# Second quarter's weight columns by direct transfers of three queues, its row cleared earlier, and the middle of each transform moved into a spare half bank

## The chip, the cores and the metric

The kernel runs on one core of a Trainium2 chip. The metric is the device time of the launch in microseconds (us); smaller is better. A run's median is compared, and the profile is of one further execution.

## The reference, cut to what matters

```python
def _attn_ref(x):                       # x: (8, 3008, 256) float32
    X = np.fft.fft(x, axis=1)
    X = np.fft.fft(X, axis=2)
    return X.real.astype(np.float32)

def _moe_ref(x, w_in, w_out):           # x: (24064, 256); w_in: (256, 2048); w_out: (2048, 256)
    h = x @ w_in
    g = h * np.cos(h)
    return (g @ w_out).astype(np.float32)
```

The output of the first is reshaped to 24064 rows and is the input of the second.

## The kernel before, in words

**The two parts.** The first part is a Fourier transform written as matmuls. Each of the 8 batches is folded (sums and differences of mirrored rows and columns), multiplied with small cosine and sine matrices (tiles `pz`, `pm` and `pb` in PSUM), and passes through DRAM (`zd`) to be turned. The second part runs over steps. A step is one batch, one of 6 groups of up to 256 columns of the transformed input, and one of 8 pairs of 128-row blocks of `w_in`. A step has two halves, `u` = 0 and 1, so there are 8 x 6 x 8 x 2 = 768 half-steps, numbered `k`. The transform's last matmul is folded into the weights: `w_in`, in four quarters of 512 columns, is multiplied with a cosine and a sine matrix (`CS`) in the opening, into `WC` and `WS`. `weights(e, q)` does that on TensorE in the tile `pw`, and `keep_weights` copies it out on VectorE.

**The row and the columns.** Row 0 of `WS` is used in another way than the rest: it must stand as columns, one per 128-row block, in the tile `wn` (16 columns, four for each quarter). Then row 0 of `WS` is set to zero (`clear_wn`, on GpSimd, L653) before TensorE multiplies with it. Before the change the four quarters get their columns in three ways: quarter 0 by four direct transfers from SBUF to SBUF (L998, two by SyncE, two by GpSimd); quarter 1 by four small matmuls that turn the row (`turn_wn`, L634) and a copy on VectorE (`keep_wn`, L644); quarters 2 and 3 by a transfer to DRAM and one back (`send_wn` L650, `load_wn` L656).

**A half-step.** ScalarE writes `nb * wn[:, f] + 0.25` into a PSUM tile `H` (`seed`, L707), TensorE adds two matmuls (`mm1`, L726, with `WC` and then `WS`), ScalarE doubles (`act_e`, L738), VectorE makes the mirrored half (`dve_h`, L742), ScalarE rounds (`act_round`, L754), VectorE takes the fraction (`dve_frac`, L758), ScalarE takes the sine (`act_sin`, L764), and VectorE multiplies (`dve_g`, L768). After two halves GpSimd forms sums and differences of the blocks (`sums`, L784 to L791, tile `S`). Seven matmuls a step, `mm2` (L817, tile `M`), multiply by `w_out`, whose blocks are combined in advance on GpSimd (`combine_w2`, L692). Seven sums need three and a half PSUM banks: the second half of the fourth `M` bank is not used. `mm2` of a step runs five to six half-steps after its first half.

**The order.** The program is written in one order, and each engine keeps its own part of it. So an instruction that waits holds whatever stands behind it on its engine, DMA issues included. `H` has four banks in turn, and `M` four. The other transforms' matmuls borrow `H` banks that are free for a moment (`borrow`).

**The middle of a transform.** For batches 1 to 7, the matmuls of a transform are set between those of the batch before it. `pairs` lists at which step a `pair_half` runs (TensorE into `pz`, then ScalarE copies by `keep_z`). Three half-steps after the first pair of a batch, `middle` (L456) multiplies the middle rows and the ends: ten small passes into `pm`, which VectorE has first set to zero (`clear_middle`, L442), and ScalarE copies it to `zm` (L1096).

**Loads and stores of the opening.** SyncE's queue carries, in this order around the change: columns 1 and 3 of quarter 0; quarters 2 and 3 of `w_in` (`load_w`); half of `w_out` (`load_w2`); eight stores of `z` (`store_z`, L473); the rest of `w_out` and a part of the matrix `BJ`; the third quarter's row (`send_wn(2)`); loads of `z` (`load_z`, L506); `load_wn(2)`. `keep_busy` (L672) issues matmuls on ones whose result nobody reads, while TensorE would wait.

Of the kernel before, what the change touches and what calls it, by code (L numbers as in the profile page):

```python
# [131 lines left out]
def kernel(  # L132
# [7 lines left out]
    nc = tc.nc  # L140
# [106 lines left out]
    def load_bj(c0, c1, eng=nc.sync):  # L247
        eng.dma_start(out=BJ[:, c0:c1], in_=B_dr.ap()[:, c0:c1])
# [4 lines left out]
    def load_w2(f0, f1, eng=nc.sync):  # L253
        eng.dma_start(
            out=w2.rearrange("p (q c) -> p q c", c=ND)[:, 2 * f0 : 2 * f1],
            in_=moe_w_out.rearrange("(q p) c -> p q c", p=128)[:, 2 * f0 : 2 * f1],
        )
# [9 lines left out]
    WS = cpool.tile([128, NDFF], FP, tag="WS", name="WS")  # L267
# [12 lines left out]
    def borrow(name, k=0):  # L280
        return ppool.tile([128, 512], FP, tag=f"H{(turn[0] + k) % 4}", bufs=1, name=name)
# [155 lines left out]
        small.append(dict(out=zv[:, 0, :, 0], in_=zr[:, :, 0]))  # L437
        small.append(dict(out=zv[:, 1, :, 0].rearrange("y (q s) -> y q s", s=2), in_=zq[:, p]))

    def clear_middle():  # L440
        pm = borrow("pm")[:, 0:144]
        nc.vector.memset(pm, 0.0)  # L442
        return pm

    def middle(pm):
        xv = xm.rearrange("r (q h s) -> r h q s", h=2, s=2)
        LZ, LM, LE0, LO0 = (L2[:, 64 * q : 64 * q + 64] for q in range(4))
# [20 lines left out]
    def store_z(p, j0=0, j1=NJ, engs=(nc.sync, nc.sync)):  # L468
        half, q = divmod(p, 2)
        zd, zs = take_zd(0, half), zps[p][:, 0:1024]  # L470
        for e in range(2):
            p0 = 16 * e + XP * q
            engs[e].dma_start(  # L473
                out=zd[p0 : p0 + XP, 256 * j0 : 256 * j1].rearrange("i (y d) -> y i d", d=128),
                in_=zs[64 * e + 2 * j0 : 64 * e + 2 * j1, :].rearrange("y (i d) -> y i d", d=128),
            )
# [82 lines left out]

    doubles = {}  # L560
    pairs = {}
    middles = set()
    per = NG * 8

    def transform(b):
        todo = {}

        def at(o, *call):
            todo.setdefault(o, []).append(call)

        for p in range(4):
            sh = (5, 3, 3, 0)[p] if b == 1 else 5 if p == 0 else 0
            o = 8 * p + sh
            if p < 2:
                at(2 if b == 1 else p, turn_x, b, p)
            at(1 + p if b > 1 else max(2, 1 + p), load_xx, b, p)
            at(5 + p + (3 if b == 1 else 0), take_middle, b, p)
            for k in range(2):
                at(o + 6 + k, fold_x, b, p, k)
                at(o + 9 + k, fold_z, b, p, k)  # L580
            pairs[per * (b - 1) + o + 9] = b, p
            at(o + 11, patch_z, b, p)
            at(o + 12, store_pair, b, p)
            if p == 0:
                for e in range(2):
                    at(10 + e, fold_ends, e)
                middles.add(per * (b - 1) + o + 10)
                at(o + 12, store_ends, b)
        at(23, load_z, b, 0)
        at(39, load_z, b, 1)  # L590
        for i in range(3):
            doubles[per * (b - 1) + (44, 46, 47)[i]] = b, (2 * i, 2 * i + 1)
        return todo
# [34 lines left out]
        W = WS if e else WC  # L628
        copy(out=W[:, 512 * n : 512 * n + 512], in_=pw)

    def turn_wn(n, pw):
        for k in range(4):
            f = 512 * n + 128 * k
            nc.tensor.matmul(  # L634
                pw[:, k : k + 1],
                lhsT=WS[0:1, f : f + 128],
                rhs=ones[0:1, 0:1],
                start=k == 0,
                stop=True,
                skip_group_check=True,  # L640
            )

    def keep_wn(n, pw):
        copy_v(out=wn[:, 4 * n : 4 * n + 4], in_=pw[:, 0:4])  # L644

    wds = {}

# [343 lines left out]
    copy_v(out=wrow, in_=WS[0:1, 0:256])  # L991
    pw.append(weights(0, 0, "H"))
    keep_weights(0, 0, pw[1], copy_v)
    for n in (512, 256):
        keep_busy(pds[0], n, False)
    for k in range(4):
        eng = nc.sync if k % 2 else nc.gpsimd
        eng.dma_start(out=wn[:, k : k + 1], in_=WS[0:1, 128 * k : 128 * k + 128])  # L998
    clear_wn(0)
    for q in (2, 3):  # L1000
        load_w(q)
    load_w2(0, 2)
    load_w2(2, 4)
    for p in (1, 2, 0, 3):
        store_z(p, 4)
    load_w2(4, 6)
    load_bj(256, 512)
    load_w2(6, 8)
    opening = {
        0: ((combine_w2, 0, 2), (clear_wn, 1)),  # L1010
        2: ((load_bj, 512, NJ * 64), (combine_w2, 2, 4)),
        3: ((combine_w2, 4, 6, 0, 2),),
        4: ((combine_w2, 4, 6, 2, 4), (load_z, 0, 0, 8), (load_z, 0, 1, 8)),
# [34 lines left out]
    for k in range(2 * n + LAG):  # L1048
        t, u = divmod(k, 2)
        d, v = divmod(k - LAG, 2)  # L1050
        cur, prev, old, nxt = unit(k), unit(k - 1), unit(k - 2), unit(k + 1)
        done = step(d)
        full = step(d if v else d - 1, True)
        if cur:
            if k % (2 * per) == 0:
                todo = transform(cur.s.b + 1) if cur.s.b + 1 < NB else {}
            if k >= AHEAD:
                mm1(cur, 0)
                act_e(cur)
            if k == 0:  # L1060
                for h in (cur, nxt):
                    mm1(h, 0)
                    seed_first(h)
                    act_e(h)
                spread_nb(0)
            if k < AHEAD - 1:
                mm1(cur, 1)
        pair = None if u else pairs.pop(t, None)
        double = None if u else doubles.pop(t, None)
        pm = clear_middle() if u and t in middles else None  # L1070
        if old:
            dve_g(old)
            if old.u:
                sums(old.s)
        if done:
            order = (0, 1, 5, 4, 3, 2, 6) if done is steps[-1] else range(7)
            mm2(done, 4 * v, 4 * v + (1 if pair or double else 3), order)
        if pair:
            pz = [borrow("pz"), borrow("pz", 1)]
            for q in range(2):  # L1080
                pair_half(*pair, q, pz[q])
            mm2(done, 4 * v + 1, 4 * v + 3, order)
        if double:
            pbs = [borrow("pb"), borrow("pb", 1)]
            kept = second_half(*double, pbs)
            mm2(done, 4 * v + 1, 4 * v + 3, order)
        if pm is not None:
            middle(pm)
        if full and full is not steps[-1]:
            take_m(full, 1 if v else 3, nc.vector)  # L1090
        if nxt and 0 < k < AHEAD - 1:
            seed(nxt)
        if prev:
            act_round(prev)
        if pm is not None:
            nc.scalar.copy(out=zm, in_=pm)  # L1096
        if pair:
            keep_z(*pair, 0, pz[0])
        if double:
            keep_b(double[1], kept[0], 0, pbs[0])  # L1100
        if nxt and k >= AHEAD - 1:
            seed(nxt)
        if full and full is not steps[-1]:
            take_m(full, 0 if v else 2, nc.scalar)
        if prev:
            dve_frac(prev)
        if k + 1 in range(2, AHEAD):
            mm1(nxt, 0)
            act_e(nxt)
        if k < 5:  # L1110
            pw.append(weights(*((1, 1), (0, 1), (1, 2), (0, 2), (1, 3))[k]))
        if k == 4:
            pw.append(weights(0, 3))
        if k == 1:
            turn_wn(1, pw[2])
        copy_small()
        if prev:
            act_sin(prev)
        if pair:
            keep_z(*pair, 1, pz[1])  # L1120
        if double:
            keep_b(double[1], kept[0], 1, pbs[1])
            if double != (0, (1,)):
                send_nb(double[1], *kept)
        if cur and k >= AHEAD - 1:
            mm1(cur, 1)
        if done and v == 0:
            mm2(done, 3, 4, order)
        if cur:
            dve_h(cur)  # L1130
        if k < 6:
            e, q = ((1, 1), (0, 1), (1, 2), (0, 2), (1, 3), (0, 3))[k]
            keep_weights(e, q, pw[k + 2], copy_v)
        if k == 1:
            keep_wn(1, pw[2])
        if k == 2:
            send_wn(2)
            load_z(0, 0, 4, 8)
            load_wn(2)
            load_z(0, 1, 4, 8)  # L1140
        if k == 4:
            send_wn(3)
            nc.sync.dma_start(out=L2, in_=L2_dr.ap())
            load_wn(3)
        if k in (5, 7):
            clear_wn((k - 1) // 2)
        if k < 2:
            for o in range(2):
                mix_weights(2 + k, o, nc.gpsimd)
        if u == 0:  # L1150
            continue
        for i in range(6):
            s = step(t - 4 - i, True)
            if s:
                combine_m(s, i)
        for sg, lag in ((0, 8), (1, 10)):
            s = step(t - lag, True)
            if s:
                store_out(s, sg)
        for call in opening.pop(t, ()):  # L1160
            call[0](*call[1:])
        for call in todo.pop(t % per, ()):
            call[0](*call[1:])
# [31 lines left out]
```

## Time and profile before

| | us |
|---|---|
| median of 3 runs | 1917.05 (1915.54 to 1918.67) |
| the profiled execution | 1915.97 |
| its span, first to last instruction | 1914.2 |
| mean granted TensorE clock | 0.999 |

The profile names engines PE (TensorE), PEld (its weight loads), DVE (VectorE), ACT (ScalarE), POOL (GpSimd) and SP (SyncE); a `q` behind the name is the engine's queue of DMA issues. A line of the timeline has the start, the duration, the engine, the source line, the operation, output and inputs with shapes, the number of instructions merged, and in brackets how long the engine had been idle and who ended that. A float32 matmul shows as two passes.

### The profile page before, as it was taken

To read this page: it belongs to the slowest core of one execution; us is meant where nothing else is said; L and a number is where in the kernel's file an instruction comes from. 1 tells how busy PE (TensorE), PEld (TensorE's weight loads), DVE (VectorE), ACT (ScalarE), POOL (GpSimd) and SP (SyncE) were. 2 spreads that over 40 slices of the span, in tenths; PEclk is the share of its full clock that TensorE was granted. 3 is DMA by queue.
4 is the path that set the end of the run, shared out by engine and by line. 5 is a ranking of instruction groups with operands and counts; after the bars stand their busy time and mean duration, and the time that the engine had idled before them with its cause. 6 is when DMAs were issued, how large, how long until landed. Compare 5 with 4: busy or idle time off the path is not lost.

```text
span 1914.2 us, 32347 instructions
## 1 busy us (share of the span) xinstructions
PE 1904.4 (99%) x10410; PEld 1658.9 (87%) x10410; DVE 1463.8 (76%) x2543; ACT 1493.3 (78%) x3354; POOL 1442.3 (75%) x1784
## 2 busy tenths in 40 slices
PE   9999999999999999999999999999999999999998
PEld 4988889888988889888898888988889888898887
DVE  6777777778777777777777777777777777788787
ACT  3777777778787777788777887778777887778775
POOL 6878768887688776888768886688867888666775
PEclk9999999999999999999999999999999999999999
DMA  7612224122231224221252212502116021210001
GB/s 209 162 30 38 49 60 110 27 42 42 73 92 30 40 41 103 61 44 30 40 123 43 46 24 41 142 21 50 29 34 151 16 51 23 40 25 14 12 15 30
DMA packets 173222, 107.96 MB, mean 56 GB/s; under 512 B 112928, under 2 KB 152702, under 8 KB 171984
## 3 DMA queue, kind: packets, MB, share of 16 engines
q1 hardware_dynamic: 170488, 103.33, 24.0%
q8 instruction: 84, 1.38, 0.3%
q10 hardware_dynamic: 1848, 1.28, 0.3%
q0 software_dynamic: 720, 1.30, 0.2%
q14 instruction: 82, 0.67, 0.1%
HBM read 68.59 MB, written 48.39 MB: 61 GB/s over the span
## 4 chain that ended last, share of the span: by engine, by line
PE 99%; DMA 1%; DVE 0%; POOL 0%; issue 0%; ACTq 0%; ACT 0%; SPq 0%; POOLq 0%; DVEq 0%
PE M L817 60%; PE H L726 34%; PE pz L403 2%; PE pb L521 2%; DMA xp<-in_x_dram 0%; PE pz L323 0%; PE pw L618 0%; PE pm L456 0%; DMA z<-zd 0%; DMA zd<-zs 0%; DVE cb L885 0%; PE H L713 0%; PE po L915 0%; POOL xf L306 0%; PE pn L557 0%
## 5 line engine op out<-in xcount | busy, mean ns | idle before, releaser
L784 POOL TENSOR_TENSOR S<-r 128x512 f32<-128x512 f32 (+1 forms) x383 | 474.9, 1240 | 380.4 <-DVE r L768 317.7
L764 ACT ACTIVATE r<-r 128x512 f32<-128x512 f32 (+1 forms) x768 | 476.6, 621 | 246.4 <-DVE r L758 244.5
L758 DVE SCALAR_TENSOR_TENSOR r<-r,H 128x512 f32<-128x512 f32 (+1 forms) x768 | 518.9, 676 | 158.3 <-ACT r L754 133.4
L817 PE MATMUL M<-S,VX 128*128 128x256 f32 (+1 forms) x2304 | 626.6, 377 | 0.0
L768 DVE SCALAR_TENSOR_TENSOR r<-H,r 128x512 f32<-128x512 f32 (+1 forms) x768 | 519.0, 676 | 121.1 <-ACT r L764 79.3
L817 PEld LDWEIGHTS M<-S,VX 128*128 128x128 f32 x2304 | 434.0, 190 | 71.2 <-issue 22.7
L726 PE MATMUL H<-pq,WC 128*128 128x256 f32 (+1 forms) x1536 | 453.3, 377 | 0.0
L726 PE MATMUL H<-pq,WS 128*128 128x256 f32 (+1 forms) x1536 | 451.7, 376 | 0.6 <-POOL WS L653 0.6
L754 ACT ACTIVATE r<-H 128x512 f32<-128x512 f32 (+1 forms) x768 | 447.4, 583 | 0.2 <-DVE H L742 0.2
L742 DVE TENSOR_TENSOR H<-ew,H 128x256 f32<-128x256 f32 (+1 forms) x768 | 324.9, 423 | 147.3 <-PE H L726 90.9
L817 PE MATMUL M<-r,w 128*128 128x256 f32 (+1 forms) x1536 | 388.0, 375 | 0.0
L707 ACT ACTIVATE H<-nb,wn 128x256 f32<-128x256 f32 (+1 forms) x766 | 365.9, 478 | 2.0
L738 ACT ACTIVATE ew<-H 128x256 f32<-128x256 f32 (+1 forms) x768 | 287.2, 374 | 99.4 <-PE H L726 95.1
L817 PEld LDWEIGHTS M<-r,w 128*128 128x128 f32 x1536 | 300.6, 197 | 27.7 <-PE pw L618 0.8
L726 PEld LDWEIGHTS H<-pq,WC 128*128 128x128 f32 x1536 | 283.4, 190 | 45.2 <-ACT H L707 7.6
L726 PEld LDWEIGHTS H<-pq,WS 128*128 128x128 f32 x1536 | 290.0, 190 | 36.0 <-POOL WS L653 1.5
L790 POOL TENSOR_TENSOR S<-S,r 128x256 f32<-128x256 f32 (+1 forms) x383 | 275.4, 719 | 30.1
L791 POOL TENSOR_TENSOR S<-r,S 128x256 f32<-128x256 f32 (+1 forms) x383 | 274.8, 718 | 30.0
L817 PE MATMUL M<-r,VX 128*128 128x256 f32 (+1 forms) x768 | 225.4, 375 | 0.0
L817 PE MATMUL M<-S,w 128*128 128x256 f32 (+1 forms) x768 | 225.4, 375 | 0.0
L817 PEld LDWEIGHTS M<-S,w 128*128 128x128 f32 x768 | 150.5, 196 | 14.4
L817 PEld LDWEIGHTS M<-r,VX 128*128 128x128 f32 x768 | 146.0, 190 | 14.4
(95 smaller groups left out, 887.1 us busy)
## 6 DMA issues: line engine op xcount, KB each, us to landing
out_dram<-ob SPq DMA_DIRECT2D x724, 32.0 KB
xp<-in_x_dram SPq DMA_DIRECT2D x119, 128.0 KB
xp<-xr SPq DMA_DIRECT2D x112, 128.0 KB
z<-zd SPq DMA_DIRECT2D x56, 192.0 KB
xr<-in_x_dram SPq DMA_DIRECT2D x14, 752.0 KB
zd<-zs SPq DMA_DIRECT2D x98, 96.0 KB
nb<-nd SPq DMA_DIRECT2D x23, 256.0 KB
wr<-in_moe_w_in_dram SPq DMA_DIRECT2D x4, 512.0 KB
```

What stands on the lines that cost most here:

```text
L707: nc.scalar.activation(out=h.H[:, 0:T], in_=s.nb[:, 0:T], func=AF.Copy, bias=0.25, scale=wn[:, f : f + 1])
L726: nc.tensor.matmul(h.H[:, 0:T], lhsT=W[:, 128 * f : 128 * f + 128], rhs=s.pq[:, e * 256 : e * 256 + T], start=False, stop=True, skip_group ...
L738: nc.scalar.mul(out=h.ew[:, 0:T], in_=h.H[:, 0:T], mul=2.0)
L742: nc.vector.tensor_tensor(out=h.H[:, T : 2 * T][:, ::-1], in0=h.ew[:, 0:T], in1=h.H[:, 0:T], op=ALU.subtract)
L754: nc.scalar.activation(out=r, in_=y, func=AF.Copy, bias=BIG, scale=1.0)
L758: nc.vector.scalar_tensor_tensor(out=r, in0=r, scalar=-BIG, in1=y, op0=ALU.add, op1=ALU.subtract)
L764: nc.scalar.activation(out=r, in_=r, func=AF.Sin, bias=0.0, scale=SIN_SCALE)
L768: nc.vector.scalar_tensor_tensor(out=r, in0=y, scalar=-0.25, in1=r, op0=ALU.add, op1=ALU.mult)
L784: tt(out=sv[:, 0:2], in0=qv[:, 1:2].to_broadcast([128, 2, T]), in1=qv[:, 0:4:3], op=ALU.subtract,)
L790: tt(out=sv[:, 2], in0=sv[:, 1], in1=gv[:, 0, 0], op=ALU.subtract)
L791: tt(out=sv[:, 3], in0=gv[:, 1, 0], in1=sv[:, 2], op=ALU.add)
L817: nc.tensor.matmul(acc[key][m // 2][:, 256 * (m % 2) : 256 * (m % 2) + T], lhsT=w, rhs=a, start=first, stop=s.fp == 7, skip_group_check=True,)
```

## The change

- Quarter 1's columns (4 to 7 of `wn`) come by four direct transfers: column 4 by ScalarE, 6 and 7 by SyncE, 5 by GpSimd. They are issued in half-step 0, after the row is copied out. The turning matmuls and their copy go.
- `clear_wn(1)` stands at the end of half-step 1 ahead of `combine_w2(0, 2)`, not behind it.
- Six of the eight stores of `z`, two loads of `w_out` and one of `BJ` move on SyncE's queue behind columns 6 and 7.
- One more filler matmul of 512 columns stands ahead of the first steps.
- The middle of a transform is computed directly behind the first pair of its batch, three half-steps earlier, into the spare half of the fourth `M` bank. The memset of `pm` goes. In that step the last of the seven sums is taken ahead of the pair.

```diff
--- before.py
+++ after.py
@@ -437,11 +437,6 @@
         small.append(dict(out=zv[:, 0, :, 0], in_=zr[:, :, 0]))
         small.append(dict(out=zv[:, 1, :, 0].rearrange("y (q s) -> y q s", s=2), in_=zq[:, p]))
 
-    def clear_middle():
-        pm = borrow("pm")[:, 0:144]
-        nc.vector.memset(pm, 0.0)
-        return pm
-
     def middle(pm):
         xv = xm.rearrange("r (q h s) -> r h q s", h=2, s=2)
         LZ, LM, LE0, LO0 = (L2[:, 64 * q : 64 * q + 64] for q in range(4))
@@ -559,7 +554,6 @@
 
     doubles = {}
     pairs = {}
-    middles = set()
     per = NG * 8
 
     def transform(b):
@@ -584,7 +578,6 @@
             if p == 0:
                 for e in range(2):
                     at(10 + e, fold_ends, e)
-                middles.add(per * (b - 1) + o + 10)
                 at(o + 12, store_ends, b)
         at(23, load_z, b, 0)
         at(39, load_z, b, 1)
@@ -628,20 +621,8 @@
         W = WS if e else WC
         copy(out=W[:, 512 * n : 512 * n + 512], in_=pw)
 
-    def turn_wn(n, pw):
-        for k in range(4):
-            f = 512 * n + 128 * k
-            nc.tensor.matmul(
-                pw[:, k : k + 1],
-                lhsT=WS[0:1, f : f + 128],
-                rhs=ones[0:1, 0:1],
-                start=k == 0,
-                stop=True,
-                skip_group_check=True,
-            )
-
-    def keep_wn(n, pw):
-        copy_v(out=wn[:, 4 * n : 4 * n + 4], in_=pw[:, 0:4])
+    def move_wn(k, eng):
+        eng.dma_start(out=wn[:, k : k + 1], in_=WS[0:1, 128 * k : 128 * k + 128])
 
     wds = {}
 
@@ -991,23 +972,18 @@
     copy_v(out=wrow, in_=WS[0:1, 0:256])
     pw.append(weights(0, 0, "H"))
     keep_weights(0, 0, pw[1], copy_v)
-    for n in (512, 256):
+    for n in (512, 512, 256):
         keep_busy(pds[0], n, False)
     for k in range(4):
-        eng = nc.sync if k % 2 else nc.gpsimd
-        eng.dma_start(out=wn[:, k : k + 1], in_=WS[0:1, 128 * k : 128 * k + 128])
+        move_wn(k, nc.sync if k % 2 else nc.gpsimd)
     clear_wn(0)
     for q in (2, 3):
         load_w(q)
     load_w2(0, 2)
     load_w2(2, 4)
-    for p in (1, 2, 0, 3):
-        store_z(p, 4)
-    load_w2(4, 6)
-    load_bj(256, 512)
-    load_w2(6, 8)
+    store_z(1, 4)
     opening = {
-        0: ((combine_w2, 0, 2), (clear_wn, 1)),
+        0: ((combine_w2, 0, 2),),
         2: ((load_bj, 512, NJ * 64), (combine_w2, 2, 4)),
         3: ((combine_w2, 4, 6, 0, 2),),
         4: ((combine_w2, 4, 6, 2, 4), (load_z, 0, 0, 8), (load_z, 0, 1, 8)),
@@ -1067,35 +1043,37 @@
                 mm1(cur, 1)
         pair = None if u else pairs.pop(t, None)
         double = None if u else doubles.pop(t, None)
-        pm = clear_middle() if u and t in middles else None
         if old:
             dve_g(old)
             if old.u:
                 sums(old.s)
         if done:
             order = (0, 1, 5, 4, 3, 2, 6) if done is steps[-1] else range(7)
+            if pair and pair[1] == 0:
+                order = (0, 1, 2, 3, 6, 4, 5)
             mm2(done, 4 * v, 4 * v + (1 if pair or double else 3), order)
         if pair:
             pz = [borrow("pz"), borrow("pz", 1)]
             for q in range(2):
                 pair_half(*pair, q, pz[q])
+            if pair[1] == 0:
+                pm = acc[done.b, done.grp][3][:, 256:400]
+                middle(pm)
             mm2(done, 4 * v + 1, 4 * v + 3, order)
         if double:
             pbs = [borrow("pb"), borrow("pb", 1)]
             kept = second_half(*double, pbs)
             mm2(done, 4 * v + 1, 4 * v + 3, order)
-        if pm is not None:
-            middle(pm)
         if full and full is not steps[-1]:
             take_m(full, 1 if v else 3, nc.vector)
         if nxt and 0 < k < AHEAD - 1:
             seed(nxt)
         if prev:
             act_round(prev)
-        if pm is not None:
-            nc.scalar.copy(out=zm, in_=pm)
         if pair:
             keep_z(*pair, 0, pz[0])
+            if pair[1] == 0:
+                nc.scalar.copy(out=zm, in_=pm)
         if double:
             keep_b(double[1], kept[0], 0, pbs[0])
         if nxt and k >= AHEAD - 1:
@@ -1111,8 +1089,6 @@
             pw.append(weights(*((1, 1), (0, 1), (1, 2), (0, 2), (1, 3))[k]))
         if k == 4:
             pw.append(weights(0, 3))
-        if k == 1:
-            turn_wn(1, pw[2])
         copy_small()
         if prev:
             act_sin(prev)
@@ -1131,8 +1107,15 @@
         if k < 6:
             e, q = ((1, 1), (0, 1), (1, 2), (0, 2), (1, 3), (0, 3))[k]
             keep_weights(e, q, pw[k + 2], copy_v)
-        if k == 1:
-            keep_wn(1, pw[2])
+        if k == 0:
+            move_wn(4, nc.scalar)
+            for i in (6, 7):
+                move_wn(i, nc.sync)
+            for p in (2, 0, 3):
+                store_z(p, 4)
+            load_w2(4, 6)
+            load_bj(256, 512)
+            load_w2(6, 8)
         if k == 2:
             send_wn(2)
             load_z(0, 0, 4, 8)
@@ -1147,6 +1130,10 @@
         if k < 2:
             for o in range(2):
                 mix_weights(2 + k, o, nc.gpsimd)
+        if k == 0:
+            move_wn(5, nc.gpsimd)
+        if k == 1:
+            clear_wn(1)
         if u == 0:
             continue
         for i in range(6):
```

## The prediction

> **What bounds the kernel now.** First the page: the busy shares, and the chain that ended last.
>
> ```profile
> PE 1904.4 (99%) x10410; PEld 1658.9 (87%) x10410; DVE 1463.8 (76%) x2543; ACT 1493.3 (78%) x3354; POOL 1442.3 (75%) x1784
> PE 99%; DMA 1%; DVE 0%; POOL 0%; issue 0%; ACTq 0%; ACT 0%; SPq 0%; POOLq 0%; DVEq 0%
> ```
>
> TensorE never rests once the steps run, so only what puts work on it or makes it wait counts; other engines' work is free while it comes in time. Then the timeline of TensorE in the opening, where the columns of weights change hands.
>
> ```profile
> 31.72 0.65 PE L726 MATMUL H<-pq,WS 128*128 128x225 f32 x2
> 32.20 0.54 PE L726 MATMUL H<-pq,WC 128*128 128x225 f32 x2
> 32.68 1.08 PE L618 MATMUL pw<-wr,CS 128*64 128x512 f32 x4
> 33.69 1.05 PE L634 MATMUL pw<-ones,WS 1*128 1x1 f32 x8
> 34.66 0.65 PE L726 MATMUL H<-pq,WS 128*128 128x225 f32 x2
> ...
> 39.26 0.65 PE L726 MATMUL H<-pq,WS 128*128 128x225 f32 x2 [0.59 <-POOL WS L653]
> ```
>
> The turned row (L634) holds TensorE from 33.69 to 34.66, 0.97 us, and at 39.26 it waits 0.59 us for the cleared row. The same stretch on the other engines:
>
> ```profile
> 30.24 0.35 ACT L558 COPY nb<-pn 128x225 f32<-128x225 f32 x1
> 30.62 0.45 ACT L707 ACTIVATE H<-nb,wn 128x225 f32<-128x225 f32 x1
> 31.86 0.69 DVE L629 COPY WS<-pw 128x512 f32<-128x512 f32 x1 [0.65 <-PE pw L618]
> ...
> 38.69 0.51 POOL L653 MEMSET WS<- 1x512 f32 x1
> ```
>
> ScalarE seeds half 2 at 30.62, before VectorE has the second quarter's row ready (31.86 + 0.69 = 32.55). Third, the middle of a transform, once in each of 7 batches:
>
> ```profile
> 105.54 0.59 PE L817 MATMUL M<-r,VX 128*128 128x256 f32 x2
> 106.06 0.30 PE L456 MATMUL pm<-xm,L 128*64 128x16 f32 x4
> 106.20 0.53 PE L456 MATMUL pm<-xzf,L 128*64 128x128 f32 x6
> 106.67 0.70 PE L726 MATMUL H<-pq,WS 128*128 128x256 f32 x2
> 107.20 0.59 PE L817 MATMUL M<-S,VX 128*128 128x256 f32 x2
> ```
>
> Two undisturbed passes take 0.43 us, so 105.97 to 106.67 is the middle's, and 0.10 us more is lost in the pair after it (0.53 instead of 0.43).
>
> **The change part by part.** Sums are against the profiled execution: span 1914.20 us, 1.77 us around it, own time 1915.97, which is 1.08 below the median of the three runs (1917.05).
>
> *The turned row and its copy leave.* TensorE −0.97 us; the copy on VectorE (0.16) lies beside other work: 0.
>
> *Column 4 is sent by ScalarE.* In half-step 0 the send follows VectorE's copy of the row, and on ScalarE it stands ahead of half 2's seed. ScalarE is free at 30.59 and would wait until 32.55; queued behind are seed 2, the rounding and the sine of half 0, and TensorE waits for the seed. No row shows this form from ScalarE; SyncE's sends of the same shape (L998) take 0.50 to 0.58 us and ScalarE's other sends 0.36 to 0.60 in the opening; I take 0.55. So the seed runs 33.15 to 33.6, the first matmul of half 2 moves from 32.20 to 33.7: +1.5. Behind it come the four matmuls of the next weights (1.0), no turned row, and half 2's second matmul at 35.2 instead of 34.66: +0.55. ScalarE stays late, since its rounding (0.55), doubling (0.36) and sine (0.58) now run one after the other with a VectorE pass between them: seed 3 ends at 36.0, so half 3 starts at 36.1 against 35.15; seed 4 ends at 38.5, half 4 starts at 38.55 against 37.11. Half 4's second matmul comes at 40.05 against 39.26, as the 0.59 for the cleared row is gone, half 5 at 40.85 against 39.74, and the sums of w_out at 43.2 against 42.08. There ScalarE has gaps (1.15 us before 43.13, 0.97 before 44.68) and the lag grows no more. Opening, all told: +1.1 us. Bounds: −0.1 (1.5 lost once, 0.97 and 0.59 gained, ScalarE catching up at once) to +2.2 (a send twice as long, its lag carried through).
>
> *Columns 6 and 7 by SyncE, column 5 by GpSimd, the row cleared early.* SyncE's two sends wait for 32.55 too, and behind them are now six stores of z, two loads of w2, one of BJ, then the third quarter's row.
>
> ```profile
> 32.92 1.27 SPq L473 DMA_DIRECT2D zd<-zs  x1
> 40.11 0.31 SPq L650 DMA_DIRECT2D wd<-WS  x1
> 43.99 0.38 SPq L656 DMA_DIRECT2D wn<-wd  x1
> ```
>
> A store costs SyncE about 0.45 us (29.48, 30.00) until the queues are full (2.40 at 30.48, then 1.1 each; DMA 94 to 98% busy from 32 to 36 us). Two stores end at 30.46, the two columns go out by 33.7, and six stores at 0.45 to 1.06 end between 36.4 and 40.1, where before they ended at 37.96: the third row's send moves by 0 to 2.2 us; I take 0.7, since the queues drain on while SyncE waits. It landed 3.9 us after its send; then its load goes out (44.7), landing by some 2.3 to 3.7 us later: 47.0 to 48.4. Seed 8 ran at 47.31 and is due at 48.4 now: 0, at the worst bound +1.6. GpSimd's send (0.57) delays its mixing of the last quarter to 36.5, needed at 40.2: 0. Clearing waits for all four columns: GpSimd's landed in 3.7 us, so 37.1, SyncE's, behind full queues, in some 3.9: by 38; the clear (0.51) is in time for 40.05. combine_w2 (2.9 us) moves behind it and ends at 41.4 instead of 38.75; the first sums end then at 42.5, needed at 44.8: 0, cover 2.3 us.
>
> *One more filler matmul of 512 columns.* Two passes of 0.43 us, under TensorE's 1.05 us wait for z before 26.16: 0; without that cover 0.86.
>
> *The middle moves* into the spare half of the fourth M bank, right behind pz. Now it costs 0.09 (start), 0.60 (106.06 to 106.66), 0.10 (after) and, for a seed held back by its copy to zm, 0.09: 0.88 us. Between pz and M the weight loads wait until pz is through ("0.81 <-issue"). If that holds between pz (64*64) and pm (128*64) too, the middle adds its 0.60 and shares both edges with pz: 0.28 saved, 7 times: −2.0 us. No row shows this pair of shapes. Bounds: 0.09 saved (both edges stay) to 0.44 (pz's tail is overlapped too; a pair of passes lasts 0.59 at a pace of 0.43, so 0.16): −0.6 to −3.1. The Trainium skill (TensorEngine Tiling (Array Packing), Key Properties) says that a change of tiling mode, not of tile, drains the array; by it the 0.28 would stand and the overlap would not, which no row here shows.
>
> *What goes with it.* Seven memsets of 0.18 us on VectorE: 0. The copy to zm (0.28 us) now stands between pz's copy and the next seed; the second pair's seed ended at 335.08 and its matmul began at 335.35; with the middle ahead, the seed ends at 335.4 and the matmul is due at 335.9: 0, cover 0.5 us a time. Taking sum 6 first needs the last part of S; that was written by 329.87 for a matmul at 332.29: 0.
>
> Sum: +1.1 − 2.0 = −0.9 us: 1915.07 as a profiled execution, 1916.15 beside the median. A measurement of this kernel tells about 0.2%, 3.8 us, from no change: no change.
>
> **The rivals.** *Faster.* ScalarE's wait is hidden. For it: ScalarE has gaps of 1.0 and 1.2 us between 31.8 and 35.7, and only if the row were ready by about 31, or a send did not hold what follows, would seed 2 be in time. Against: 30.59 to 32.55 is twice its nearest gap. Then the opening gives −0.97 − 0.59 and the middle its full −3.1: −4.7, so 1912.4 beside the median. Chance 0.17.
>
> *Slower: what SyncE sends for the seeds lands late.* Place: its queue between 30.5 and 48 us. All that leaves SyncE after the columns is late together, and loading columns 8 to 11 needs a send and a landing first. For it: full queues at 28 to 36 and 40 to 44 us, 3.9 us for 2 KB. Against: the first landing has 4 us to spare, the others about half a microsecond. It decides when columns 8 to 11 land after 48.4 us; each microsecond more is one on TensorE, and ScalarE's queue stands with it. At the bounds worked out above (sent at 42.4, on hand at 46.3, landed at 50.0) it costs 1.6: sum +0.7. Past the limit of 3.8 it must be at 53.1; one more landing of 3.9 us on that bound makes 53.9, so 1.1 + 5.5 − 2.0 = +4.6: 1921.6. Chance 0.29.
>
> *The mode change takes all of the middle's gain* (−0.6) and the opening its upper bound (+2.2): +1.6, 1918.7; this is still no change.
>
> **How the numbers follow.** No change 0.54, with its own range from 1913.8 (opening −0.1, middle −3.1) to 1918.7; faster 0.17, slower 0.29. Leaving out about 0.09 below and 0.11 above, the range reaches halfway into both rivals: 1912.6 to 1921.0.
>
> **What would show it.** Right: no L634; a send on ScalarE's queue starting near 32.6 and TensorE idle about 1.5 us before half 2; no wait for L653 near 40; the sums of w_out beginning near 43.2; pm directly behind pz, with 0.60 us of its own. Wrong: TensorE waiting for a seed at 47 to 50 us, for S ahead of the pair, or for the copy to zm; the sums of w_out beginning before 42; the granted clock under 1.00 after the wait at 32 us.

## The result, and the profile after

The changed kernel takes 1920.15 us (median of 22 runs, 1919.07 to 1923.82); the kernel before takes 1916.99 (22 runs). The ratio is 1.0017, 95% interval [1.0011, 1.0023]: slower by about 3.2 us. The forecast was 1916.15 us and no change; the time lies inside the stated range, and the loss is under the 0.2% that was called no change, but with this many runs it is clear of noise and has the other sign.

The first three lines are from the page of the changed kernel (span, busy shares, chain by engine); the rest is what TensorE waited for in its trace (total, times, longest).

```profile
span 1917.3 us, 32328 instructions
PE 1903.4 (99%) x10404; PEld 1658.4 (86%) x10404; DVE 1462.6 (76%) x2535; ACT 1493.8 (78%) x3354; POOL 1442.2 (75%) x1785
PE 95%; POOL 3%; DVE 1%; issue 1%; DMA 0%; ACT 0%; ACTq 0%; POOLq 0%; DVEq 0%
PE pz L403 <- POOL xf L384: 4.6, 6, 0.8
PE H L707 <- ACT H L688: 1.6, 2, 1.4
```

TensorE has 1.0 us less work, and the span is 3.1 us longer. GpSimd (POOL) has come into the chain that ended last, with 3% of it. The second wait is the forecast one in the opening. The first is new: in six of the seven batches the matmuls of a pair, `pz`, wait for GpSimd's last fold, `xf` (L384), 0.77 us each. In the kernel before, TensorE waited for nothing between 45 us and the last outputs.

The pair that waits is not the one behind which the middle was put, but the next, three steps later. This is GpSimd between the two pairs of batch 2, in the kernel before, with TensorE's old middle and its second pair below:

```profile
336.71 1.28 POOL L784 TENSOR_TENSOR S<-r 128x512 f32<-128x512 f32 x1 [0.76 <-DVE r L768]
...
340.17 1.41 POOL L426 TENSOR_TENSOR zs<-zr 128x252 f32<-128x252 f32 x2
...
346.23 1.41 POOL L426 TENSOR_TENSOR zs<-zr 128x252 f32<-128x252 f32 x2
347.60 1.27 POOL L377 TENSOR_TENSOR xf<-xp 128x512 f32<-128x512 f32 x1
348.95 0.21 POOL L384 TENSOR_TENSOR xf<-xp 128x4 f32<-128x4 f32 x1
...
341.91 0.29 PE L456 MATMUL pm<-xm,L 128*64 128x16 f32 x4
342.05 0.53 PE L456 MATMUL pm<-xzf,L 128*64 128x128 f32 x6
...
349.27 1.19 PE L403 MATMUL pz<-xf,L 64*64 64x512 f32 x8
```

and in the changed kernel, with TensorE below:

```profile
337.27 1.27 POOL L765 TENSOR_TENSOR S<-r 128x512 f32<-128x512 f32 x1 [1.37 <-DVE r L749]
...
349.53 0.21 POOL L384 TENSOR_TENSOR xf<-xp 128x4 f32<-128x4 f32 x1
...
348.43 0.59 PE L798 MATMUL M<-S,VX 128*128 128x256 f32 x2
349.79 1.09 PE L403 MATMUL pz<-xf,L 64*64 64x512 f32 x8 [0.77 <-POOL xf L384]
```

In the kernel before, no bracket stands on any of GpSimd's lines after the first: from 336.71 to 349.16 it works without a gap, and the second pair begins at 349.27, 0.11 us after that fold. In this stretch GpSimd was the bound all along, and the old middle's 0.88 us of TensorE time lay inside it at no cost. The change takes the middle out of the stretch, so TensorE is through earlier, and puts it ahead of the stretch, so that the work on which GpSimd's stretch starts comes 0.56 us later (337.27 against 336.71). At the second pair, TensorE is ready 0.25 us earlier than before (349.79 − 0.77 = 349.02, against 349.27) and the pair starts 0.52 us later (349.79): together the 0.77. This reading is put to the test below.

### The profile page after: what moved, and what is told of

Its sections match the earlier page's. It is cut to its first block, busy times and chain, and to the rows that moved or that the text cites. A ratio compares the mean times of both kernels' runs of the same rounds, so it can differ in the third digit from the quotient of the medians.

```text
span 1917.3 us, 32328 instructions
## 1 busy us (share of the span) xinstructions
PE 1903.4 (99%) x10404; PEld 1658.4 (86%) x10404; DVE 1462.6 (76%) x2535; ACT 1493.8 (78%) x3354; POOL 1442.2 (75%) x1785
## 3 DMA queue, kind: packets, MB, share of 16 engines
q0 software_dynamic: 752, 1.31, 0.2%
## 4 chain that ended last, share of the span: by engine, by line
PE 95%; POOL 3%; DVE 1%; issue 1%; DMA 0%; ACT 0%; ACTq 0%; POOLq 0%; DVEq 0%
PE M L798 57%; PE H L707 33%; PE pz L403 2%; PE pb L516 2%; POOL zs L426 1%; POOL S L765 1%; PE pd L653 1%; POOL S L771 0%; POOL S L772 0%; POOL xf L377 0%; PE pw L611 0%; PE pz L323 0%; PE M L451 0%; DVE r L749 0%; POOL cb L849 0%
## 5 line engine op out<-in xcount | busy, mean ns | idle before, releaser
L688 ACT ACTIVATE H<-nb,wn 128x256 f32<-128x256 f32 (+1 forms) x766 | 365.9, 478 | 4.4 <-DVE WS L622 2.7
```

Source lines behind the costliest of these rows:

```text
L688: nc.scalar.activation(out=h.H[:, 0:T], in_=s.nb[:, 0:T], func=AF.Copy, bias=0.25, scale=wn[:, f : f + 1])
```

## The experiments

Two theories were set against each other at first: G, that GpSimd's unbroken stretch between the first two pairs is the bound there; and O, that the opening made the loss. The column on the right is the distance between the starts of `pb` in the third and fourth transforms, worked out from each trace (before: 950.04 − 715.75).

| kernel | median us | ratio to before | one batch, us |
|---|---|---|---|
| before | 1916.99 | | 234.29 |
| the change | 1920.15 | 1.0017 [1.0011, 1.0023] | 234.74 |
| e1 opening only | 1917.30 | 1.0001 [0.9992, 1.0009] | 234.29 |
| e2 middle only | 1919.50 | 1.0012 [1.0003, 1.0021] | 234.80 |
| e3 change, second pair 1 step later | 1918.34 | 1.0007 [0.9998, 1.0016] | 234.46 |
| e4 change, column 4 by SyncE | 1921.00 | 1.0015 [1.0006, 1.0024] | 234.76 |
| e5 before, no middle | 1915.19 | 0.9990 [0.9982, 0.9999] | 234.13 |
| e6 no middle, pairs apart | 1911.89 | 0.9970 [0.9959, 0.9981] | 233.63 |
| e7 middle moved, pairs apart | 1917.38 | 0.9998 [0.9989, 1.0007] | 234.24 |
| e8 before, pairs apart | 1918.10 | 1.0005 [0.9996, 1.0014] | 234.52 |
| e9 middle moved, folds later | 1915.67 | 0.9989 [0.9980, 0.9998] | 234.01 |
| e10 change, folds later | 1915.90 | 0.9992 [0.9983, 1.0001] | 234.00 |
| e11 best try | 1913.89 | 0.9980 [0.9972, 0.9989] | 234.01 |
| e12 before, folds later | 1916.81 | 1.0000 [0.9991, 1.0009] | 234.29 |
| e13 best try and filler | 1914.08 | 0.9984 [0.9975, 0.9993] | 234.01 |
| e14 before and filler | 1916.83 | 0.9995 [0.9986, 1.0004] | 234.28 |
| e15 e10 without filler | 1915.80 | 0.9996 [0.9987, 1.0004] | 234.00 |

**The halves of the change, apart.** e1 puts the middle back as it was; e2 makes only the middle's edit in the kernel before.

```diff
--- the changed kernel
+++ e1
+        pm = clear_middle() if u and t in middles else None
...
-            if pair[1] == 0:
-                pm = acc[done.b, done.grp][3][:, 256:400]
-                middle(pm)
...
+        if pm is not None:
+            middle(pm)
```

> The changed kernel with the middle put back (memset, borrowed bank, three half-steps after the first pair). Theory G (GpSimd is the bound between the first and the second pair of a batch, and the middle that stood between them cost nothing there): 0.3 us over the kernel before, as the opening of the changed trace is (42.35 against 42.08 at the first sum of w_out), so about 1917.3, and no wait of pz for xf of 0.8 us. Rival O (the opening made the loss, through transfers or queues that come late): about 1920, like the changed kernel.

> The kernel before with the middle alone moved as in the change. Theory G: batches 2 to 7 lose about 0.47 us each and batch 1 gains 0.29: 6 x 0.47 - 0.29 = +2.5, so about 1919.5, with six waits of pz for xf of about 0.77 us. Rival O: -2.0, the 0.28 us saved at each of 7 middles, so about 1915.

Measured: 1917.30 and 1919.50, as theory G had it. The wait for `xf` stands in e2's trace and not in e1's:

```profile
PE pz L403 <- POOL xf L384: 4.7, 6, 0.8
```

The loss is the middle's; rival O falls, though e1's interval leaves the opening anything from −1.5 to +1.7 us.

**Is it GpSimd's stretch, or the middle's matmuls?** e5 leaves the middle out of the kernel before; e6 does so and sets the pairs further apart.

```diff
--- before
+++ e5
-        pm = clear_middle() if u and t in middles else None
+        pm = None
...
--- e5
+++ e6
-            sh = (5, 3, 3, 0)[p] if b == 1 else 5 if p == 0 else 0
+            sh = (5, 3, 3, 0)[p]
```

> The kernel before without the middle: the memset, the matmuls of pm and the copy to zm are left out in all 7 batches (zm holds zeros). Theory G (GpSimd's unbroken work from the sums after the first pair to the fold for the second is the bound there): the 0.88 us of TensorE are gained in batch 1 only, where the second pair comes three steps later; in batches 2 to 7 pz waits for xf about 0.8 us instead: 0.9 to 1.5 us below the kernel before, about 1915.8. Rival F (TensorE is the bound all the way): 7 x 0.88 = 6.2 below, about 1910.8, and no wait for xf.

> The run without the middle, and in batches 2 to 7 the second and third pair three steps later, as batch 1 has them (GpSimd gets three more steps between the first two pairs). Theory G: now the whole 7 x 0.88 = 6.2 us are gained: about 1910.8, no wait for xf. Rival F: the same as the run without the middle, since the pairs' place is of no account.

Measured: 1915.19, so taking away 6.2 us of TensorE time gained 1.8, and in its place stands

```profile
PE pz L404 <- POOL xf L385: 4.5, 6, 0.8
```

With the pairs apart that wait is gone and the time falls to 1911.89, 5.1 below the kernel before. Rival F (TensorE bound all the way) had 1910.8 for both. So the old middle ran under GpSimd's time. The remaining 1.1 to the forecast of e6 is the price of the pairs' new place:

> The kernel before, with only the second and third pair of batches 2 to 7 three steps later, the middle untouched. Control: by theory G there is about 0.1 us a batch to gain, as the middle already gives GpSimd its time: within 0.7 us of the kernel before. If the pairs' place alone gains 2 us, the middle's move is not what the run with both shows.

> The kernel before with the middle moved as in the change, and in batches 2 to 7 the second and third pair three steps later. Theory G, and no clash with the transposes of the output as at one step later: 7 x 0.28 = 2.0 us below the kernel before, about 1915.0, each batch 234.0 us instead of 234.3, no wait for xf. If the middle's move costs something else as well: not below the kernel before.

```diff
--- e7: e2, e8: before
+++
-            sh = (5, 3, 3, 0)[p] if b == 1 else 5 if p == 0 else 0
+            sh = (5, 3, 3, 0)[p]
```

The control e8 took 1918.10 and 0.23 us more a batch, e7 1917.38. Both are misses: theory G had e8 within 0.7 of the kernel before and slightly gaining, and e7 2.0 below it, where it came out level. Only the difference between the two fits: the batch differs by 234.52 − 234.24 = 0.28, just what the middle's move was to save, but the pairs' new place, which theory G had at no price, takes 0.23 of it away. There `pz` lasts 1.31 us instead of 1.20, twice a batch:

```profile
363.45 0.69 DVE L768 SCALAR_TENSOR_TENSOR r<-H,r 128x512 f32<-128x512 f32 x1 [0.24 <-ACT r L764]
363.96 1.31 PE L403 MATMUL pz<-xf,L 64*64 64x512 f32 x8
```

`pz` borrows two `H` banks, and the second comes free only when VectorE's product (L768) has read it, at 364.14; singly, the first matmul into it starts at 364.19, 0.23 us behind the one into the first bank, against 0.12 in the kernel before. At this step of a group VectorE is late. One step later instead of three, as in e3, it was worse:

```diff
--- the changed kernel
+++ e3
-            sh = (5, 3, 3, 0)[p] if b == 1 else 5 if p == 0 else 0
+            sh = (5, 3, 3, 0)[p] if b == 1 else (5, 1, 0, 0)[p]
```

> The changed kernel, with the second pair of batches 2 to 7, its folds and its stores one step later (GpSimd gets one more step of about 4.75 us between the two pairs). Theory G: the six waits of 0.77 us go, 4.6 us less than the changed kernel: about 1915.5, which is 1.5 below the kernel before. Rival T (the loss is TensorE's own: another order of the sums, the middle's writes into a bank in use): stays at about 1920.

```profile
354.04 0.71 DVE L918 STREAM_TRANSPOSE ob<-cb 128x512 f32<-128x512 f32 x1
354.68 0.65 DVE L749 SCALAR_TENSOR_TENSOR r<-H,r 128x512 f32<-128x512 f32 x1
354.83 1.63 PE L403 MATMUL pz<-xf,L 64*64 64x512 f32 x8
```

The six waits for `xf` went, but 1918.34 is 2.8 above the forecast: the transpose of the output (L918) stands ahead of that product, and `pz` lasts 1.63 us, 0.43 more a batch; its second bank starts at 355.39, 0.06 us after that product ends. Rival T, that nothing changes, does not fit either (1.8 us below the changed kernel), and e9 and e10, with the middle where the change has it, rule it out.

**Give GpSimd time without moving the pairs.** e9, e10 and e12 move GpSimd's two folds of the first pair's result two steps later, behind the second pair's folds, in batches 2 to 7.

```diff
+            w = 2 if b > 1 and p == 0 else 0
...
-                at(o + 9 + k, fold_z, b, p, k)
+                at(o + 9 + k + w, fold_z, b, p, k)
...
-            at(o + 11, patch_z, b, p)
-            at(o + 12, store_pair, b, p)
+            at(o + 11 + w, patch_z, b, p)
+            at(o + 12 + w, store_pair, b, p)
```

> The kernel before with the middle moved as in the change, and in batches 2 to 7 GpSimd's two folds of the first pair's result (fold_z, 1.41 us each), with their patch and store, two steps later, so that they do not stand between the first and the second pair; the pairs stay where they were. Theory G: GpSimd is 2.8 us early for the second pair, no wait for xf, and the middle's 0.28 us are gained 7 times: a batch takes 234.0 us instead of 234.29, 2.0 below the kernel before, about 1915.0. If it is not GpSimd's amount of work in that stretch but the start of it: the wait of 0.77 us stays, about 1919.5.

> The whole change, with the same two folds two steps later. Theory G: the six waits of 0.77 us go: about 4.6 us below the changed kernel, 1915.5. If the opening had a loss of its own that the waits covered: above 1917.

> The kernel before with only the folds two steps later, the middle untouched. Control: the second pair had about 0.1 us to wait at most, so theory G gives at most 0.7 us: between 1916.3 and 1917.0. If this alone gains 2 us, the middle's place is of no account.

Measured: 1915.67, 1915.90 and 1916.81, each within 0.7 us of theory G. In e9 the fold is through before TensorE asks for it, and nothing waits:

```profile
346.90 0.21 POOL L384 TENSOR_TENSOR xf<-xp 128x4 f32<-128x4 f32 x1
348.25 0.59 PE L811 MATMUL M<-S,VX 128*128 128x256 f32 x2
348.78 1.19 PE L403 MATMUL pz<-xf,L 64*64 64x512 f32 x8
```

The edit turns the whole change from +3.2 us to a gain of 1.1 against the 1916.99 of the table, or 1.5 against the runs of before that were taken beside it (the interval of e10 just touches 1), while for the kernel before the same edit is worth nothing. So neither the middle's new place nor the folds' place decides alone, but what GpSimd has to do between the pairs.

**The opening.** e4 sends column 4 by SyncE.

```diff
--- the changed kernel
+++ e4
-            move_wn(4, nc.scalar)
-            for i in (6, 7):
+            for i in (4, 6, 7):
                 move_wn(i, nc.sync)
```

> The changed kernel with column 4 sent by SyncE too, so that ScalarE's queue holds no send. If ScalarE's wait for the second quarter's row is what the opening loses: the waits of 1.41 and 0.16 us for the seeds of halves 2 and 4 go and SyncE is 0.5 us later: 1.0 to 1.6 us below the changed kernel, about 1918.8, and the first sum of w_out near 41. If the columns' landing is the limit: the seed of half 4 waits for it, and nothing is gained.

The waits of 1.41 and 0.16 us went, and another came: the seed of half 4 (ScalarE, L688) waits for its column.

```profile
31.70 2.05 SPq L625 DMA_DIRECT2D wn<-WS  x3
36.75 0.45 ACT L688 ACTIVATE H<-nb,wn 128x225 f32<-128x225 f32 x1 [1.46 <-DMA wn<-WS]
37.25 0.65 PE L707 MATMUL H<-pq,WC 128*128 128x225 f32 x2 [1.81 <-ACT H L688]
```

From the first send at 31.70, which is column 4's, to the seed are 5.0 us, with TensorE 0.4 us ahead of where the changed kernel had it. The landing is the limit behind the send: 1921.00, nothing gained.

**The best version.** e11 is e9 with the row cleared early, as in the change, and the turned row kept.

```diff
--- e9
+++ e11
-        0: ((combine_w2, 0, 2), (clear_wn, 1)),
+        0: ((combine_w2, 0, 2),),
...
+        if k == 1:
+            clear_wn(1)
```

> The kernel before with the middle moved, the folds two steps later, the turned row of the second quarter kept, and the row cleared ahead of w_out's sums of weights as in the change. Expected: 2.0 from the middle and 0.6 from the wait for the cleared row: about 1914.4. If the wait only passes on to the next thing in the opening: as the run without the early clear, about 1915.0.

1913.89, 3.6 us below its own runs of before (ratio 0.9980 [0.9972, 0.9989]), faster than both kernels. That is 1.8 us below e9, where 0.6 was expected of the early clear. The wait that the early clear takes away was 0.59 us in the profile of before but up to 1.79 in others (see the opening, below), which would account for it; no run shows that it does.

**The filler.** In four profiles with the opening of before or of e11 (e6, e7, e11, e12) the granted clock fell for a few us between 30 and 36 us, in none with the opening of the change. That does not mean that it never falls there: 7 of the 22 executions of the changed kernel, those of 1921.89 us and more, have a mean granted clock of only 0.996 or 0.997, with that opening and its filler. e13 (e11 with it), e14 (before with it) and e15 (e10 without it) try the filler matmul by itself:

```diff
-    for n in (512, 256):
+    for n in (512, 512, 256):
```

> The best try so far (turned row kept, row cleared early, middle moved, folds two steps later) with the change's extra filler matmul of 512 columns. If the filler keeps the clock up in the opening: granted clock 1.00 throughout and 0.5 to 1.5 us below that try, 1912.4 to 1913.4. If the filler is only more work: 0 to 0.9 above it, about 1914.3.

> The kernel before with the extra filler matmul alone. If the filler keeps the clock up: clock 1.00 throughout in the profile, and the median 0.3 to 1.0 below the kernel before with less scatter (before: 1915.2 to 1920.6). If it is only more work under a wait: the same median within 0.3.

> The change with the folds two steps later, without its extra filler matmul. If the filler keeps the clock up: 0.3 to 1.0 above the same kernel with it (1915.9), more scatter, a granted clock near 0.6 at 30 to 34 us in some executions. If not: 1915.9 or up to 0.9 below.

1914.08, 1916.83 and 1915.80: each pair is the same within its noise (+0.2, −0.3, −0.1). The clock was 1.00 in all three profiles, without the filler too. The filler has no share in the result that could be measured, and why the clock falls in some executions stays open. One sign is common to the four: TensorE waits 0.62 to 1.24 us for the cleared row before its first matmul with `WS`, near 30 us, and in none of the other thirteen profiles does it wait there.

## Why the prediction was wrong

*The middle: the step that failed.* The forecast had −2.0 us, "0.28 saved, 7 times". The saving itself was right: in batch 1, where the second pair is six steps away, the distance from the first pair to the next batch's first pair fell by 0.30 (235.86 to 235.56), and e9 and e10 save 0.28 in the batch of the table. What was left out is what the 0.88 us had covered. The forecast looked for cover of the operations that it moved (the copy to zm, sum 6, the memset) and called TensorE the bound because its busy share was 99%; it did not ask what TensorE was about to wait for had the middle not been there. The row that told it was in the trace of before: GpSimd's fold ended at 349.16 and the pair began at 349.27. Instead of −0.28 a batch, six batches lost 0.77 − 0.28, on average 0.47 as measured (0.16 to 0.82 singly, since in each of the two traces one batch takes some 0.36 us more than its neighbours, and not the same one; why is open): 6 x 0.47 − 0.30 = +2.5, and e2 measured +2.5.

*The shape of the middle behind `pz`* was right. This view has the weight loads (PEld) and matmuls of the changed kernel:

```profile
332.78 1.20 PE L403 MATMUL pz<-xf,L 64*64 64x512 f32 x8
333.91 0.20 PEld L451 LDWEIGHTS M<-xm,L 128*64 128x64 f32 x4 [0.81 <-issue]
...
334.05 0.53 PE L451 MATMUL M<-xzf,L 128*64 128x128 f32 x6
334.51 1.13 PE L798 MATMUL M<-S,VX 128*128 128x256 f32 x4
```

The middle's weights wait until `pz` is through (0.81 us), and it takes 333.91 to 334.51, 0.60. The Trainium skill (TensorEngine Tiling (Array Packing), Key Properties) says that a change of mode drains the array; for 64*64 to 128*64 the trace now agrees, and the end of the range with an overlap (0.44) is out.

*The opening* was right in its mechanism; its size, +1.1, was half again what the two profiles show.

```profile
31.28 0.65 PE L707 MATMUL H<-pq,WS 128*128 128x225 f32 x2
33.34 0.65 PE L707 MATMUL H<-pq,WC 128*128 128x225 f32 x2 [1.41 <-ACT H L688]
...
37.80 0.65 PE L707 MATMUL H<-pq,WC 128*128 128x225 f32 x2 [0.16 <-ACT H L688]
...
42.35 1.03 PE L798 MATMUL M<-r,w 128*128 128x225 f32 x4
...
32.15 0.58 ACTq L625 DMA_DIRECT2D wn<-WS  x1
32.83 0.45 ACT L688 ACTIVATE H<-nb,wn 128x225 f32<-128x225 f32 x1 [2.69 <-DVE WS L622]
```

ScalarE's queue waits for the row, sends (0.58; 0.55 was taken), and seeds half 2 at 32.83; TensorE waits 1.41 us, 1.5 forecast. From half 1 to the first sum of w_out it takes 42.35 − 31.28 = 11.07 us against 10.36 before: +0.71 instead of +1.1, since ScalarE caught up one half-step earlier (waits of 1.41, 0, 0.16). But the 10.36 are one execution's. The wait for the cleared row, taken at 0.59, is 1.59, 1.60 and 1.79 us in e8, e14 and e2, which have the opening of before, and the stretch takes 11.36, 11.37 and 11.57 us there; with the opening of the change it takes 11.06 to 11.08 in five profiles. Against those three executions the change's opening is the shorter one, by 0.3 to 0.5. So one profile could not give this term, and its sign stays open: the whole opening measured +0.3 in e1, with an interval that holds +0.7 and −0.5. The wait for the cleared row went, as forecast, and the filler lay under the wait for z.

*The rivals.* Faster did not come: ScalarE's wait was not hidden. The slower rival named SyncE's late sends; columns 8 to 11 were late by 0.25 us at one seed and TensorE lost nothing by it. That the time still lies inside the stated range is owed to the range's width, which was set for other reasons. The sign of the slower rival came true by another mechanism, which was on nobody's list: a wait that takes the place of the work removed, on an engine with a busy share of 75%.

## What to carry to other kernels

Before work is taken off the busiest engine, look at what that engine would reach next and when its input is ready; if the input is ready only just in time, as here 0.11 us ahead, the work taken away was free. An engine at 75% on average can be the bound for a stretch of 12 us, and the sign of it is a run of lines without brackets that ends right at a start on the other engine. Here the time freed was worth something only together with the edit that gave the other engine time: the middle's move alone cost 2.5 us, and with two folds deferred (e9) it gained about 1.3.

## What the runs showed of the hardware

The granted TensorE clock fell without a long wait. In e12, stretches of 2 us show 0.56 from 32 to 34 us and 0.59 from 34 to 36, after a wait of 1.24 us that ended at 30.80; in e11 0.58 and 0.57 from 30 to 34, after a wait of 0.62. In e7 the stretch from 32 to 34 shows 0.50. At half speed the loss in e11 is 2 x (0.42 + 0.43) / 0.5 = 3.4 us, and the stretches of e6, e7 and e12 give the same. In e2 and e14 waits of 1.8 and 1.6 us, some 10 us later, left the clock at 1.00. The Trainium skill (TensorE: Matmul & The Clock Gate, The HAM clock gate) gives 3.4 us as the length of its window, which the 3.4 us of half speed agree with; it asks for a whole idle window before the clock falls, which the waits of 0.62 and 1.24 us do not bear out.
